# Scanning one decay product once for all blocks in a fused scan and SwiGLU kernel on one Trainium2 core

## The chip, the cores and the metric

One Trainium2 chip, one of its cores. Five engines run their own instruction streams and meet by semaphores: TensorE (PE, matmuls), VectorE (DVE), ScalarE (ACT), GpSimd (POOL) and SyncE (SP, which only issues transfers here). The metric is the device time of one launch in microseconds (us).

## What is computed

```python
# batch 4, heads H 8, seq 768, head_dim 32, d_state N 16; chunk 32
log_a = log(clip(a, 1e-6, 1));  cum = cumsum(log_a within the chunk)
M = (C_i . B_j) * exp(cum_i - cum_j) for j <= i          # in the chunk
y = M x + (C_i . state) * exp(cum_i)
state = exp(sum log_a) * state + sum_j exp(cum_end - cum_j) B_j x_j
# then, with x = y as 3072 tokens x 256 and DFF = 1536
out = (silu(x @ w_gate) * (x @ w_val)) @ w_out
```

All of it is float32. Two kinds of decay products are needed: those that multiply scores and B (called `aj` in the kernel, tile `L`) and those that multiply C (called `an`, tile `E`).

## The kernel before, in words

**Tiling.** The sequence is cut into NB = 6 blocks of P = 128 positions; a block of all four batches is T = 512 tokens. In a block the scan works on K = 2 pieces of Q = 64 positions. DFF is cut into NF = 12 units of 128. For each block PE computes, in this order of meaning: the sums for the states (`st <- xb`), the scores (`S <- Cz, bc`), the outputs of the scan (`y <- L, xb` for what lies in the piece and `y <- bc, T` for the state's part), then for each unit f the gate and the value (`gv`, two matmul groups, gate and value), and from the products the output (`po`). Blocks 4 and 5 are done together with fewer products (`px, py, pz, pr`, then `ox, oy, oz, or`), and so are the last eight units of block 3 in another form (`hx, hy, hz`).

**Weights.** They arrive as 64-bit patterns (`wNr`) that are turned into floats by a chain on two engines: `w_magnitude` (ACT, `wNw <- wNr`), `w_sign` and `w_rest` (ACT, `wNr <- wNr`; the rest partly on DVE), `w_range`, `w_shift` and `w_round` (DVE). In block 0 the units f < `WHOLE` multiply with the whole float32 weight (`gv <- xf, wNw`: two matmuls for the gate and two for the value). Every other unit uses a split into a high and a low fp32r part (`wNh`, cast on ACT, and `wNl`, a subtraction on DVE), and x split likewise (`xh`, and `hhx`, `hlx` for the low half in block 0), six matmuls each for gate and value. `gate_val` (L959) holds both ways.

**Decays.** Block 0 builds its `L` and `E` from rows that PE spreads. For blocks 1 to 5 the raw decays come in one tile `all` (`load_all`: 128 partitions, two halves `aj` and `an`, each NA x W = 3 x 65 = 195 wide), are clipped on POOL (`clip_all`), and go back to memory as `clipped` by one transfer that ACT issues (`write_all`). From there `load_aj` (two transfers a block, `L <- clipped`) and `load_an` (one, `E <- clipped`) spread them, and DVE scans them into running products: `scan_j`, four times a block, `L <- L, dj`, and `scan_n`, once a block, `E <- E, dn`, each 128 x 520. `weigh_b` multiplies B with the last decays (`xb <- xb, L`), four instructions of 128x128 a block, on POOL for block 0 and on DVE after it. `weigh_c` multiplies C (`bc <- bc, E`), `mix` the scores (`L <- S, L`), the step of the state is `T <- T, E, T` and `T <- T, E`.

**Order.** Nothing is ordered by hand. Each piece of work is added to a planner with an engine, a cost, a rank and what it needs; the planner puts it on an engine's list by its rank (a due time), and `Ordered` then fixes that list as the engine's program. All instructions are issued in that helper, L202, so every row of the trace has line 202 and is told apart by its tiles. The ranks hang on a table of numbers: `LEAD[k]` is how long before its block's units a block's scan work is due, `LATE` ties a block's loads to a weight, `AHEAD` is how early stored weights are fetched, `BEHIND` sorts the terms of the last output products, `SUM_LAG` sets the sums before them. The lines in question:

```python
add("Act", 0.45, write_all, 7.5, ["clipped"], gives="written", lag=0.6)
...
add("DVE", 1.17, do(scan_n, k), z + 6, [("an", k)], gives=("E", k), slack=1.0)
...
WHOLE = 9
```

Of the kernel before, what the change touches and what calls it, by code (L numbers as in the profile page):

```python
# [28 lines left out]
NF = DFF // P  # L29
# [14 lines left out]
class Plan:  # L44
# [26 lines left out]
    def add(self, engine, cost, run, rank, needs=(), takes=(), uses=(), gives=None, kind=None, lag=0.0, rows=1.0, slack=0.0):  # L71
        engines = [(engine, cost)] if cost is not None else engine
        self.ops.append(Op(engines, run, rank, needs, takes, uses, gives, kind, lag, rows, slack))
# [139 lines left out]
def scan_moe_kernel(ctx: ExitStack, tc, rows, decays, bc, xb, wgv, wo, cst, out):  # L213
    nc = tc.nc
    PSUM = bass.MemoryType.PSUM
    te, ve, se, ge, sp = (
        Ordered(tc, e) for e in (nc.tensor, nc.vector, nc.scalar, nc.gpsimd, nc.sync)
    )
# [18 lines left out]
    dn = const.tile([P, BATCH * K, W], F32, tag="dn", name="dn")  # L237
# [5 lines left out]
    clipped = dram.tile([2, P, NA * W], F32, name="clipped")  # L243
    bl = [dict(y={}) for _ in range(NB)]
# [50 lines left out]
        t = bl[0]["all"] = att.tile([P, 2, NA, W], F32, name="all")  # L295
        sp.dma_start(t.rearrange("p i a t -> p i (a t)"), decays.rearrange("i p c -> p i c"))

    def write_all():
        t = bl[0]["all"]
        se.dma_start(clipped.rearrange("i p c -> p i c"), t.rearrange("p i a t -> p i (a t)"))  # L300

    def load_bc(k):
        t = bl[k]["bc"] = att.tile([P, 2, BATCH, P], F32, tag="bc", name=f"bc{k}")
# [15 lines left out]
    def scan(t, d):  # L319

        ve.tensor_tensor_scan(t, t, d, 0.0, ALU.mult, ALU.add)
# [30 lines left out]
        t = bl[k]["L"][:, H * b : H * b + H]  # L352
        scan(t.rearrange("p h t -> p (h t)"), dj.rearrange("p h t -> p (h t)"))

    def scan_n(k):

        scan(bl[k]["E"].rearrange("p b q t -> p (b q t)"), dn.rearrange("p g t -> p (g t)"))


    def heads_apart(k, e):  # L360

# [6 lines left out]

    def weigh_b(k, b):

        t = bl[k]["Bj"].rearrange("p b (h n) -> p b h n", n=N)[:, b]
        L = bl[k]["L"].rearrange("p (b h) t -> p b h t", h=H)[:, b, :, Q:]
        (ve if k else ge).tensor_tensor(out=t, in0=t, in1=L.to_broadcast([P, H, N]), op=ALU.mult)

    def weigh_c(k):
        t = bl[k]["C"].rearrange("p b (q i) -> p b q i", i=Q)
# [664 lines left out]
    def do(f, *a):  # L1041
        return lambda *e: f(*a, *e)
# [6 lines left out]
    add = plan.add  # L1049

    GV, GVH, PO, ATT, FIRST, PACE0, GVP = 2.82, 2.6, 1.41, 5.0, 18.0, 3.5, 4.95
    begin, begin_sum, t = {}, {}, FIRST
# [27 lines left out]
    for n, ranks in enumerate(IDLE):  # L1080
        for i, r in enumerate(ranks):
            need = [("idle", n, i - 1)] if i else [("idle", n - 1, len(IDLE[n - 1]) - 1)] if n else []
            if n:
                need = need + [(("S", 0, BATCH - 1), ("vals", 0), ("y", 0))[n - 1]]
# [25 lines left out]

    add("SP", 0.48, load_all, 3.6, [("sent", 0)], gives="all", lag=0.6)
    add("Pool", 1.5, clip_all, 13.0, ["all", *(("bt", 0, b) for b in range(BATCH))], gives="clipped")
    add("Act", 0.45, write_all, 7.5, ["clipped"], gives="written", lag=0.6)


    for k in range(NB):
# [7 lines left out]
        def gate(key):  # L1124
            return [("asked", 1) if key in ("bc", "xb") else ("round", GATE[key])] if k == 1 else []
# [11 lines left out]
        if not k:  # L1137
            add("-", 0.0, lambda: None, -9, takes=[("x", "rows")], gives="rows", lag=0.1)
            for i in range(2):
                add("DVE", 0.2, do(clip_rows, i), -9 + i, ["rows"], gives=("clip", i))  # L1140
            for b in range(BATCH + 1):
                for i in range(2 if b < BATCH else 1):
                    t = ("spread", b, i)
                    last_one = int(i and b == BATCH - 1)
                    r = z + (3.0 if b == BATCH else 0.1 * b + i * (0.15 if b == BATCH - 1 else 0.5))
                    d = -1.09 if b == BATCH else r
                    done = ("E", 0) if b == BATCH else ("L", 0, b)
                    bank = "at" if in_at(b, i) else "mm"
                    add("PE", 0.433 if b < BATCH else 0.2, do(spread, b, i), r, [("clip", i)] + ([("S", 0, BATCH - 1)] if b == BATCH else []), takes=[(bank, t)], uses=[t, "rows"], gives=t, kind="s", slack=0.1)
                    need = [t, ("decays", 0), "dj"] + ([("scan0", b - last_one)] if i else []) + ([("M", 0, NP - 2)] if b == BATCH else [])  # L1150
                    add("DVE", 0.6, do(scan_spread, b, i), d, need, uses=[t], gives=done if i or b == BATCH else ("scan0", b))
        else:
            add("SP", 0.96, do(load_aj, k), z - 12, ["written", ("decays", k), *late, *gate("aj")], gives=("aj", k), lag={1: 5.0, 2: 11.0}.get(k, 6.0))
            plan.marked[plan.ops[-1]] = ("asked", k)
            add("SP", 0.48, do(load_an, k), z - 9, ["written", ("decays", k), *late, *gate("an")], gives=("an", k), lag=1.3)
            for b in range(BATCH):
                add("DVE", 1.14, do(scan_j, k, b), z + 0.5 + b, [("aj", k)], gives=("L", k, b), slack=2.0)
            add("DVE", 1.17, do(scan_n, k), z + 6, [("an", k)], gives=("E", k), slack=1.0)
        for b in range(BATCH):
            add(*(("DVE", 0.21) if k else ("Pool", 0.45)), do(weigh_b, k, b), z + 1.0 + b if k else -1.2, [("L", k, b), ("xb", k)], gives=("bt", k, b))  # L1160
        apart_done = [("Cz", k)]
        add([("Act", 1.25), ("DVE", 0.72)][: 1 + (k > 0)], None, do(heads_apart, k), z, [("bc", k), "cs"], takes=[("Cz", CZ)], gives=("Cz", k))
        add("DVE", 0.6 if k else 0.35, do(weigh_c, k), z + 8 if k else -1.0, [("E", k), *apart_done], gives=("ce", k))
# [3 lines left out]
        for bs in [(b,) for b in range(BATCH)] if not k else [range(BATCH)]:  # L1167
            b, more = bs[-1], bs[0]
            n = len(bs)
            stb = st[:1] if k in ST_ONE else st  # L1170
            bank = "mm" if k in ST_MM else "at"
            if k in JOINED:
                def run(k=k, bs=bs):
                    sums(k, bs)
                    scores(k, bs)
                need = [*(("bt", k, i) for i in bs), ("Cz", k)]
                add("PE", 2.04, run, z + 3, need, takes=[*((bank, i) for i in stb), *(("at", i) for i in S)], uses=[*stb, *S, CZ], gives=("S", k, BATCH - 1), kind="f", slack=SLACK)
                continue
            add("PE", 0.11 if n == 1 else 0.9, do(sums, k, bs), -1.5 if not k else z + 3, [*(("bt", k, i) for i in bs), *([("st", k, more - 1)] if more else [] if k else [("spread", BATCH - 1, 1)])], takes=[] if more else [(bank, i) for i in stb], uses=stb, gives=("st", k, b), kind="f", slack=SLACK, rows=1.0)
            add("PE", 0.214 if n == 1 else 1.25, do(scores, k, bs), z + 3.5 if k else -1.9 + 0.1 * b, ([("Cz", k), ("st", k, BATCH - 1)] if k else apart_done) + ([("S", k, more - 1)] if more else []), takes=[] if more else [("at" if k else "mm", i) for i in S], uses=[*S, CZ], gives=("S", k, b), kind="f", slack=SLACK, rows=1.0)  # L1180
        done = [("S", k, BATCH - 1)]
        add("-", 0.0, do(new_states, k), z + 2, behind("T"), takes=[("T", TT)], gives=("T", k))
# [310 lines left out]
NA = NB * K * BATCH * H // P  # L1493
IDLE = [-9.0] * 22, [-1.45] * 4, [-1.35] * 2, [1000.0] * 3
LATER = 2.4
ST_ONE, ST_MM, JOINED = (), (1, 2, 3, 4), (1, 2, 3, 4)
LEAD = {1: -26.4, 2: -36, 3: -65.3, 4: -66.7, 5: -56.2}
PAIR_LAG, MIXED, RAW = 5.0, 4, 4
MIXED_AFTER = ("y", 1)
HALVED = {3: 4}  # L1500
HALF_AT = "z"
MAKE, MAKE_STEP = 116.9, 3.3
LOOSE = {3: (3, 5, 7)}
AHEAD, URGENT = 14.6, 60


def in_raw(f):
# [2 lines left out]

OUT_MAKE, OUT_STEP = 198.7, 3.7
OUT_RAW = 1, 3, 5
BEHIND, AFTER = 0.9, 0
MORE = 3
EARLY, SUM_LAG = 7.7, 8.0
STAYS = "11", "12", "21", "22", "t1", "t2", "t4"
SPARE = ("L", 0), ("E", 0), ("bc", 0), ("xb", 0), ("Cz", 0), ("T", 0), ("T", 1), ("dj", 0), ("dn", 0), ("w", 0)
MADE = (
# [15 lines left out]
    return f >= HALVED.get(k, NF)  # L1534


WHOLE = 9
LATE = {2: NF + 2}
GATE, HASTE = dict(bc=0, aj=0, xb=0, an=1), 7
HELD = {1: ("M", 0, 0), 2: ("M", 0, 1), 3: ("M", 0, 3)}  # L1540

# [51 lines left out]
```

## Time and profile before

| | |
|---|---|
| median of 3 runs | 336.8 us (336.55 to 337.06) |
| the profiled execution | 337.27 us, of which the trace's span is 335.6 |
| PE busy | 330.7 us, 99% of the span |
| PE weight loads busy | 259.2 us, 77% |
| DVE busy | 294.8 us, 88% |
| ACT busy | 193.3 us, 58% |
| POOL busy | 4.3 us, 1% |
| granted TensorE clock | 0.998 of full |
| chain of work that ended last | PE 98%, DMA 1% |

A row of the timeline gives when an instruction started, how long it (or the xN of its kind) ran, its engine, line and operation, the tiles written and read, and in brackets the time the engine stood idle before it, with what ended that. Instructions of one engine overlap a little, so the time that one costs its engine is the distance from start to start, which is somewhat less than its duration.

### The profile page before, as it was taken

To read this page: it belongs to the slowest core of one execution; us is meant where nothing else is said; L and a number is where in the kernel's file an instruction comes from. 1 tells how busy PE (TensorE), PEld (TensorE's weight loads), DVE (VectorE), ACT (ScalarE), POOL (GpSimd) and SP (SyncE) were. 2 spreads that over 40 slices of the span, in tenths; PEclk is the share of its full clock that TensorE was granted. 3 is DMA by queue.
4 is the path that set the end of the run, shared out by engine and by line. 5 is a ranking of instruction groups with operands and counts; after the bars stand their busy time and mean duration, and the time that the engine had idled before them with its cause. 6 is when DMAs were issued, how large, how long until landed. Compare 5 with 4: busy or idle time off the path is not lost.

```text
span 335.6 us, 7902 instructions
## 1 busy us (share of the span) xinstructions
PE 330.7 (99%) x3189; PEld 259.2 (77%) x3189; DVE 294.8 (88%) x574; ACT 193.3 (58%) x360; POOL 4.3 (1%) x11
## 2 busy tenths in 40 slices
PE   8999999999999999999999999999999999999995
PEld 7544448888888888878888889988888888888784
DVE  5999999987997999887999985997578999889993
ACT  3686899276554653555455344553565556544982
POOL 1300000000000000000000000000000000000000
PEclk9999999999999999999999999999999999999999
DMA  7699749992011599277978489543036522230011
GB/s 246 185 331 343 206 127 385 289 247 64 25 33 34 163 257 368 97 278 217 274 250 305 152 279 202 188 137 118 2 125 251 190 69 69 114 125 0 1 65 63
DMA packets 21261, 57.68 MB, mean 172 GB/s; under 512 B 2280, under 2 KB 3304, under 8 KB 21224
## 3 DMA queue, kind: packets, MB, share of 16 engines
q1 hardware_dynamic: 20808, 56.94, 53.7%
q8 instruction: 25, 0.41, 0.5%
q10 hardware_dynamic: 416, 0.23, 0.2%
q14 instruction: 12, 0.10, 0.1%
HBM read 41.23 MB, written 15.93 MB: 170 GB/s over the span
## 4 chain that ended last, share of the span: by engine, by line
PE 98%; DMA 1%; ACT 0%; issue 0%; DVE 0%; ACTq 0%
PE gv L202 35%; PE po L202 20%; PE py L202 7%; PE y L202 5%; PE px L202 5%; PE oy L202 4%; PE hy L202 3%; PE pr L202 2%; PE pz L202 2%; PE ox L202 2%; PE S L202 2%; PE a L202 2%; PE hx L202 2%; PE hz L202 2%; PE st L202 1%; PE oz L202 1%
## 5 line engine op out<-in xcount | busy, mean ns | idle before, releaser
L202 ACT CAST hh<-sg 128x512 fp32r<-128x512 f32 (+1 forms) x54 | 29.2, 558 | 32.5 <-PE po L202 23.4
L202 DVE TENSOR_TENSOR hl<-sg,hh 128x512 fp32r<-128x512 f32 (+1 forms) x56 | 33.3, 607 | 7.8 <-ACT hh L202 7.5
L202 ACT ACTIVATE sg<-gv 128x512 f32<-128x512 f32 x40 | 23.8, 595 | 23.3 <-PE gv L202 19.6
L202 DVE TENSOR_TENSOR sg<-gv,sg 128x512 f32<-128x512 f32 x40 | 27.1, 678 | 2.8 <-PE gv L202 2.8
L202 DVE TENSOR_TENSOR_SCAN L<-L,dj 128x520 f32<-128x520 f32 x20 | 24.1, 1228 | 0.0
L202 DVE TENSOR_TENSOR ws<-ws 128x128 f32<-128x128 f32 (+1 forms) x60 | 19.9, 361 | 0.5 <-DMA ws<-uncut 0.4
L202 DVE TENSOR_TENSOR L<-S,L 128x512 f32<-128x512 f32 x24 | 15.7, 682 | 1.1 <-PE S L202 1.1
L202 ACT ACTIVATE sg<-px 128x512 f32<-128x512 f32 x12 | 7.2, 599 | 15.8 <-PE px L202 15.8
L202 PE MATMUL py<-xht,ws 128*128 128x512 f32 x48 | 15.3, 401 | 0.0
L202 DVE TENSOR_TENSOR hlt<-stt,hht 128x512 fp32r<-128x512 f32 x18 | 11.7, 684 | 0.9 <-ACT hht L202 0.7
L202 PEld LDWEIGHTS y<-L,xb 64*32 64x32 f32 x768 | 8.7, 105 | 4.8 <-issue 3.6
L202 ACT CAST ws<-ws 128x512 fp32r<-128x512 f32 x11 | 6.8, 622 | 8.4 <-DVE ws L202 8.2
L202 ACT ACTIVATE sg<-pz 128x512 f32<-128x512 f32 x12 | 7.2, 599 | 7.3 <-PE pz L202 7.3
L202 PE MATMUL y<-L,xb 64*32 64x64 f32 x768 | 10.9, 224 | 0.2 <-issue 0.2
L202 ACT ACTIVATE Cz<-bc,cs 128x512 f32<-128x512 f32 x12 | 8.0, 716 | 5.0 <-DMA bc<-in_bc 5.0
L202 PEld LDWEIGHTS py<-xht,ws 128*128 128x128 f32 x48 | 8.6, 188 | 2.8 <-DVE pz L202 1.2
L202 DVE TENSOR_TENSOR ps<-py,ps 128x512 f32<-128x512 f32 x12 | 8.3, 689 | 2.7 <-PE py L202 2.7
L202 ACT CAST hht<-stt 128x512 fp32r<-128x512 f32 x17 | 9.8, 622 | 0.7 <-DVE stt L202 0.6
L202 PE MATMUL py<-xlt,ws 128*128 128x512 f32 x24 | 9.4, 391 | 0.0
L202 DVE TENSOR_TENSOR pz<-py,ps 128x512 f32<-128x512 f32 x12 | 8.3, 694 | 0.7 <-PE py L202 0.4
L202 ACT COPY py<-px 128x512 f32<-128x512 f32 x12 | 6.9, 574 | 1.3
L202 PE MATMUL y<-bc,T 32*64 32x64 f32 x352 | 7.6, 223 | 0.0
(774 smaller groups left out, 979.7 us busy)
## 6 DMA issues: line engine op xcount, KB each, us to landing
ws<-keep SPq DMA_DIRECT2D x20, 512.0 KB, 4.2
keep<-ws SPq DMA_DIRECT2D x12, 512.0 KB, 5.9
L<-clipped SPq DMA_DIRECT2D x10, 520.0 KB, 10.7
xb<-in_xb SPq DMA_DIRECT2D x6, 768.0 KB, 9.4
bc<-in_bc SPq DMA_DIRECT2D x6, 512.0 KB, 10.7
ws<-uncut SPq DMA_DIRECT2D x12, 256.0 KB, 3.9
wos_k<-keep SPq DMA_DIRECT2D x6, 512.0 KB, 4.3
out<-ob SPq DMA_DIRECT2D x8, 256.0 KB, 4.7
```

Source lines behind the costliest of these rows:

```text
L202: ins = getattr(self.engine, name)(*a, **k)
```

## The change

The `an` half of `all` is scanned once, as 128 x 195, before it is written (`scan_all`, DVE), in place of a scan of each block's spread tile (`scan_n` is gone, and `load_an` now brings the finished products). `write_all` becomes two transfers, the second after that scan. `weigh_b` of blocks 1 to 5 becomes one instruction over all four batches, which needs all four scans of `L`. `WHOLE` goes from 9 to 8, so unit 8 of block 0 uses the split weights. Five settings that set ranks are new.

```diff
-    def write_all():
-        t = bl[0]["all"]
-        se.dma_start(clipped.rearrange("i p c -> p i c"), t.rearrange("p i a t -> p i (a t)"))
+    def scan_all():
+        t = bl[0]["all"][:, 1].rearrange("p a t -> p (a t)")
+        scan(t, dn[:, :NA].rearrange("p g t -> p (g t)"))
+
+    def write_all(i):
+        se.dma_start(clipped[i], bl[0]["all"][:, i].rearrange("p a t -> p (a t)"))
...
-    def scan_n(k):
-
-        scan(bl[k]["E"].rearrange("p b q t -> p (b q t)"), dn.rearrange("p g t -> p (g t)"))
...
-        t = bl[k]["Bj"].rearrange("p b (h n) -> p b h n", n=N)[:, b]
-        L = bl[k]["L"].rearrange("p (b h) t -> p b h t", h=H)[:, b, :, Q:]
-        (ve if k else ge).tensor_tensor(out=t, in0=t, in1=L.to_broadcast([P, H, N]), op=ALU.mult)
+        t = bl[k]["Bj"].rearrange("p b (h n) -> p b h n", n=N)
+        L = bl[k]["L"].rearrange("p (b h) t -> p b h t", h=H)[:, :, :, Q:]
+        if k:
+            ve.tensor_tensor(out=t, in0=t, in1=L.to_broadcast([P, BATCH, H, N]), op=ALU.mult)
+        else:
+            ge.tensor_tensor(out=t[:, b], in0=t[:, b], in1=L[:, b].to_broadcast([P, H, N]), op=ALU.mult)
...
-    add("Act", 0.45, write_all, 7.5, ["clipped"], gives="written", lag=0.6)
+    add("Act", 0.45, do(write_all, 0), 7.5, ["clipped"], gives=("written", 0), lag=0.6)
+    add("DVE", 0.47, scan_all, SCAN_ALL, ["clipped", ("xf", 2 * K - 1)], gives="scanned")
+    add("Act", 0.45, do(write_all, 1), 7.6, ["scanned"], gives=("written", 1), lag=0.6)
...
-            add("SP", 0.48, do(load_an, k), z - 9, ["written", ("decays", k), *late, *gate("an")], gives=("an", k), lag=1.3)
+            add("SP", 0.48, do(load_an, k), z - 9, [("written", 1), ("decays", k), *late, *gate("an")], gives=("E", k), lag=1.3)
...
-            add("DVE", 1.17, do(scan_n, k), z + 6, [("an", k)], gives=("E", k), slack=1.0)
...
+            add("DVE", 0.6, do(weigh_b, k, 0), z + 4.0, [*(("L", k, b) for b in range(BATCH)), ("xb", k)], gives=("bt", k, BATCH - 1))
...
+SCAN_ALL = 1.0
-LEAD = {1: -26.4, 2: -36, 3: -65.3, 4: -66.7, 5: -56.2}
+LEAD = {1: -27.1, 2: -40.4, 3: -64.2, 4: -67.5, 5: -56.2}
-AHEAD, URGENT = 14.6, 60
+AHEAD, URGENT = 13.1, 60
-BEHIND, AFTER = 0.9, 0
+BEHIND, AFTER = 0.6, 0
-EARLY, SUM_LAG = 7.7, 8.0
+EARLY, SUM_LAG = 7.7, 4.1
-WHOLE = 9
-LATE = {2: NF + 2}
+WHOLE = 8
+LATE = {2: NF + 1}
```

The first place is on DVE, ahead of the first units of block 0. `L202 ISA` is `w_round`, which unit 1's matmuls wait for. Before:

```order
L202 COPY xf<-y_1_263 128x4x64
L202 COPY xf<-y_1_306 128x4x64
L202 CAST xh_377<-xf 128x512 x2
L202 TENSOR_SCALAR wg1w<-wg1w 128x512
L202 TENSOR_TENSOR hhx<-xf,xh_377 128x512
L202 SCALAR_TENSOR_TENSOR wg1w<-wg1w,wg1r 128x512
L202 TENSOR_TENSOR hlx<-xf,xh_377 128x512
L202 ISA wg1w<-wg1r,wg1w 128x1024
```

And of the change:

```order
L202 COPY xf<-y_1_263 128x4x64
L202 COPY xf<-y_1_306 128x4x64
L202 SCALAR_TENSOR_TENSOR all<-all,dn 128x195
L202 CAST xh_383<-xf 128x512
L202 TENSOR_SCALAR wg1w<-wg1w 128x512
L202 CAST xh_383<-xf 128x512
L202 TENSOR_TENSOR hhx<-xf,xh_383 128x512
L202 SCALAR_TENSOR_TENSOR wg1w<-wg1w,wg1r 128x512
L202 TENSOR_TENSOR hlx<-xf,xh_383 128x512
```

The scan of `all` stands ahead of everything that unit 1's weight still needs from DVE; otherwise one cast of `xh` and the range have changed places.

The second place is on DVE later in block 0, where block 1's scores are mixed; the four `L<-S` rows are `mix`. Before:

```order
L202 SCALAR_TENSOR_TENSOR E_370<-E_370,dn 128x520
L202 TENSOR_TENSOR sg_6_530<-gv_6_1_527,sg_6_530 128x512
L202 ISA wg8w<-wg8r,wg8w 128x1024
L202 TENSOR_SCALAR wg9w<-wg9w 128x512
L202 TENSOR_TENSOR bc_391<-bc_391,E_370 128x512
L202 SCALAR_TENSOR_TENSOR wg9w<-wg9w,wg9r 128x512
L202 TENSOR_TENSOR L_369<-S_0_572,L_369 128x4x2x64
L202 SCALAR_TENSOR_TENSOR T_108<-T_107,E_370,T_108 128x64 x4
L202 TENSOR_TENSOR L_369<-S_1_573,L_369 128x4x2x64
L202 ISA wg9w<-wg9r,wg9w 128x1024
L202 TENSOR_TENSOR L_369<-S_2_574,L_369 128x4x2x64
L202 TENSOR_TENSOR sg_7_636<-gv_7_1_633,sg_7_636 128x512
```

And of the change:

```order
L202 ISA wg8w<-wg8r,wg8w 128x1024
L202 ISA wg9w<-wg9r,wg9w 128x1024
L202 TENSOR_TENSOR bc_392<-bc_392,E_370 128x512
L202 TENSOR_TENSOR L_369<-S_0_563,L_369 128x4x2x64
L202 SCALAR_TENSOR_TENSOR T_108<-T_107,E_370,T_108 128x64 x4
L202 TENSOR_TENSOR sg_6_600<-gv_6_1_609,sg_6_600 128x512
L202 TENSOR_TENSOR wg8l<-wg8w,wg8h 128x512
L202 TENSOR_TENSOR L_369<-S_1_564,L_369 128x4x2x64
L202 TENSOR_TENSOR L_369<-S_2_565,L_369 128x4x2x64
L202 SCALAR_TENSOR_TENSOR T_108<-T_108,E_370 128x64 x4
L202 TENSOR_TENSOR L_369<-S_3_566,L_369 128x4x2x64
L202 TENSOR_TENSOR sg_7_646<-gv_7_1_641,sg_7_646 128x512
```

The scan of `E` is gone, `wg8l` stands ahead of the second mix, and unit 7's product stands behind the last mix rather than ahead of it.

The third place is SP's list of transfers in the same stretch (the row with + is new there, the one with - was there before):

```order
 L202 DMA wg7r<-in_wgv 128x1024
 L202 DMA wg8r<-in_wgv 128x1024
-L202 DMA E_370<-clipped 128x1x520
 L202 DMA wg9r<-in_wgv 128x1024
 L202 DMA wg10r<-in_wgv 128x1024
 L202 DMA wg11r<-in_wgv 128x1024
+L202 DMA E_370<-clipped 128x1x520
 L202 DMA wo0r<-in_wo 128x1024
```

The spread of block 1's `E` is asked for behind three weights that it stood ahead of. On PE, the sums and scores of block 1 move from between units 6 and 7 to between unit 6's gate and value.

## Rows read from the trace of the kernel before

**Rows 1.** The page: busy time, share of the span and instructions by engine.

```profile
PE 330.7 (99%) x3189; PEld 259.2 (77%) x3189; DVE 294.8 (88%) x574; ACT 193.3 (58%) x360; POOL 4.3 (1%) x11
```

**Rows 2.** Windows: busy time by engine, clock, DMA share, GB/s.

```profile
15.00:25.00 10.00, 9.93 (x44) 4.30 (x37) 9.87 (x24) 8.99 (x17) 0.00 (x0) 1.00 0.96 313
35.00:60.00 25.00, 25.00 (x381) 15.35 (x380) 24.95 (x53) 22.35 (x45) 0.00 (x0) 1.00 0.73 242
60.00:300.00 240.00, 240.00 (x2287) 198.75 (x2287) 210.81 (x418) 126.43 (x235) 0.00 (x0) 1.00 0.55 171
```

**Rows 3.** Waits of PE: total, times, longest, in us.

```profile
PE oy L202 <- ACT oby L202: 0.5, 1, 0.5
```

**Rows 4.** Timeline of PE, units of block 0 and the first of block 1.

```profile
15.91 3.67 PE L202 MATMUL gv<-xf,wg0w 128*128 128x512 f32 x8
19.65 3.67 PE L202 MATMUL gv<-xf,wg1w 128*128 128x512 f32 x8
...
36.90 3.60 PE L202 MATMUL gv<-xf,wg6w 128*128 128x512 f32 x8
...
45.88 3.60 PE L202 MATMUL gv<-xf,wg8w 128*128 128x512 f32 x8
49.41 1.05 PE L202 MATMUL y<-L,xb 64*32 64x64 f32 x64
50.39 0.69 PE L202 MATMUL y<-bc,T 32*64 32x64 f32 x32
...
55.33 0.86 PE L202 MATMUL y<-L,xb 64*32 64x64 f32 x64
56.11 0.69 PE L202 MATMUL y<-bc,T 32*64 32x64 f32 x32
...
60.95 0.61 PE L202 MATMUL gv<-xh,wg0h 128*128 128x512 f32 x2
...
63.67 0.61 PE L202 MATMUL gv<-xh,wg1h 128*128 128x512 f32 x2
```

**Rows 5.** Timeline of DVE, ahead of unit 1 and at block 1's first scan.

```profile
15.34 0.76 DVE L202 COPY xf<-y 128x256 f32<-128x256 f32 x2
...
18.82 0.69 DVE L202 CUSTOM_DVE_ANT_0 wg1w<-wg1r,wg1w 128x1024 uint16<-128x1024 uint16 x1
...
29.70 1.23 DVE L202 TENSOR_TENSOR_SCAN L<-L,dj 128x520 f32<-128x520 f32 x1
30.85 0.67 DVE L202 TENSOR_TENSOR sg<-gv,sg 128x512 f32<-128x512 f32 x1
```

**Rows 6.** Tile E and tile xb: duration ns min/median/max, first and last start.

```profile
L202 DVE TENSOR_TENSOR_SCAN E<-E,dn x5: 1216/1229/1234, 40.4 to 218.2; 128x520 f32<-128x520 f32 x5
L202 DVE TENSOR_TENSOR_SCAN E<-a,dn x1: 689/689/689, 12.4 to 12.4; 128x260 f32<-128x260 f32 x1
...
L202 DVE TENSOR_TENSOR xb<-xb,L x20: 260/282/293, 32.4 to 218.0; 128x128 f32<-128x128 f32 x20
```

**Rows 7.** Timeline of ACT, from unit 1's weight to the first silu.

```profile
15.66 1.27 ACT L202 ACTIVATE wg1r<-wg1r 128x512 int32<-128x512 int32 x2
17.90 0.60 ACT L202 ACTIVATE sg<-gv 128x512 f32<-128x512 f32 x1 [0.97 <-PE gv L202]
```

**Rows 8.** Timeline of DVE, block 1's scores.

```profile
43.02 0.68 DVE L202 TENSOR_TENSOR bc<-bc,E 128x512 f32<-128x512 f32 x1
...
44.97 0.87 DVE L202 SCALAR_TENSOR_TENSOR T<-T,E,T 128x64 f32<-128x64 f32 x4
...
48.94 0.68 DVE L202 TENSOR_TENSOR L<-S,L 128x512 f32<-128x512 f32 x1
```

**Rows 9.** Transfers, 12 to 48 us: KB each, median us from issue to landing; SP timeline.

```profile
wg11r<-in_wgv SPq DMA_DIRECT2D x1, 512.0 KB, 11.9
wo0r<-in_wo SPq DMA_DIRECT2D x1, 512.0 KB, 3.3
...
29.49 0.33 SPq L202 DMA_DIRECT2D wg11r<-in_wgv  x1
```

More of the change, by code (lines that the diff above doesn't have):

```diff
@@ L1152, in scan_moe_kernel @@
         else:
-            add("SP", 0.96, do(load_aj, k), z - 12, ["written", ("decays", k), *late, *gate("aj")], gives=("aj", k), lag={1: 5.0, 2: 11.0}.get(k, 6.0))
+            add("SP", 0.96, do(load_aj, k), z - 12, [("written", 0), ("decays", k), *late, *gate("aj")], gives=("aj", k), lag={1: 5.0, 2: 11.0}.get(k, 6.0))
             plan.marked[plan.ops[-1]] = ("asked", k)
-            add("SP", 0.48, do(load_an, k), z - 9, ["written", ("decays", k), *late, *gate("an")], gives=("an", k), lag=1.3)
+            add("SP", 0.48, do(load_an, k), z - 9, [("written", 1), ("decays", k), *late, *gate("an")], gives=("E", k), lag=1.3)
             for b in range(BATCH):
                 add("DVE", 1.14, do(scan_j, k, b), z + 0.5 + b, [("aj", k)], gives=("L", k, b), slack=2.0)
-            add("DVE", 1.17, do(scan_n, k), z + 6, [("an", k)], gives=("E", k), slack=1.0)
-        for b in range(BATCH):
-            add(*(("DVE", 0.21) if k else ("Pool", 0.45)), do(weigh_b, k, b), z + 1.0 + b if k else -1.2, [("L", k, b), ("xb", k)], gives=("bt", k, b))
+        if k:
+            add("DVE", 0.6, do(weigh_b, k, 0), z + 4.0, [*(("L", k, b) for b in range(BATCH)), ("xb", k)], gives=("bt", k, BATCH - 1))
+        for b in range(0 if k else BATCH):
+            add("Pool", 0.45, do(weigh_b, k, b), -1.2, [("L", k, b), ("xb", k)], gives=("bt", k, b))
         apart_done = [("Cz", k)]
@@ L1175, in run @@
                     scores(k, bs)
-                need = [*(("bt", k, i) for i in bs), ("Cz", k)]
+                need = [("bt", k, BATCH - 1), ("Cz", k)]
                 add("PE", 2.04, run, z + 3, need, takes=[*((bank, i) for i in stb), *(("at", i) for i in S)], uses=[*stb, *S, CZ], gives=("S", k, BATCH - 1), kind="f", slack=SLACK)
                 continue
-            add("PE", 0.11 if n == 1 else 0.9, do(sums, k, bs), -1.5 if not k else z + 3, [*(("bt", k, i) for i in bs), *([("st", k, more - 1)] if more else [] if k else [("spread", BATCH - 1, 1)])], takes=[] if more else [(bank, i) for i in stb], uses=stb, gives=("st", k, b), kind="f", slack=SLACK, rows=1.0)
+            add("PE", 0.11 if n == 1 else 0.9, do(sums, k, bs), -1.5 if not k else z + 3, [("bt", k, b), *([("st", k, more - 1)] if more else [] if k else [("spread", BATCH - 1, 1)])], takes=[] if more else [(bank, i) for i in stb], uses=stb, gives=("st", k, b), kind="f", slack=SLACK, rows=1.0)
             add("PE", 0.214 if n == 1 else 1.25, do(scores, k, bs), z + 3.5 if k else -1.9 + 0.1 * b, ([("Cz", k), ("st", k, BATCH - 1)] if k else apart_done) + ([("S", k, more - 1)] if more else []), takes=[] if more else [("at" if k else "mm", i) for i in S], uses=[*S, CZ], gives=("S", k, b), kind="f", slack=SLACK, rows=1.0)
```

## The prediction

> **What bounds the kernel.** I read four views, in this order. The page comes first: PE is busy for 330.7 of 335.6 us, DVE for 294.8 [rows 1]. Then the windows, to see whether that is an average over stages: from 60 to 300 us PE is busy for 240.00 of 240.00 us, at a granted clock of 1.00, while DVE has 29 us to spare in them [rows 2]. Between 35 and 60 us DVE is full too, 24.95 of 25.00, and from 15 to 25 us it is at 9.87 of 10.00 [rows 2]: there the two run neck and neck, and DVE can decide. Third, the waits: the one worth a name behind 60 us is 0.5 us before the last output products, on an ACT copy [rows 3]. Last, the timeline of PE, because a matmul's busy time is modelled and its start isn't. The whole units 1 to 5 start 17.25 / 5 = 3.45 us apart, while each shows 3.60 to 3.67 us of busy time [rows 4]. Unit 1 is the exception: it starts 3.74 behind unit 0, so PE already stands some 0.29 us there. Unit 1's round on DVE starts at 18.82 and takes 0.69, to 19.51, and the matmuls start at 19.65 [rows 4, 5]: 0.14 behind it, so DVE sets that start. So PE is the path from 16 us to the end; a change counts where it alters PE's own work, and where DVE is late for it before 60 us.
>
> **What the change does, part by part.**
>
> *Unit 8 by split weights* is the one change of PE's work. A whole unit takes 3.45 from start to start; a split unit 63.67 - 60.95 = 2.72, though it has 12 matmuls for 8 [rows 4]. That is **-0.73 us**, on the path. Block 0's split units have the low half of x in two pieces of one matmul each, as units 9 to 11 have already. Moved sums, scores and y's are the same matmuls elsewhere; they cost PE nothing unless they come before their inputs.
>
> *The scan of all.* No row shows a scan 195 wide, so I go by its neighbours: 520 wide takes 1229 ns, 260 wide 689 [rows 6], so (1229 - 689) / 260 = 2.08 ns an element, and 195 wide takes 689 - 65 x 2.08 = 554 ns. From start to start a scan takes 0.08 less than its duration (29.70 to 30.85 is 1.15, for 1.23) [rows 5], which leaves 0.47. It stands right behind the copies into `xf` (15.34) and ahead of everything that unit 1's weight needs on DVE, where DVE has 0.13 us of idle time in 10 [rows 2, 5]. So unit 1's round ends at 19.51 + 0.47 = 19.98 and its matmuls start at 20.12: **+0.47**. The bounds are 0 (a gap on DVE that I don't see takes it up) and 0.61 (a scan that is not cheaper than one 260 wide: 0.689 less the 0.08). I take the value between, which is nearest to the slope of the two rows. A gain has no place here.
>
> *The second write* waits on ACT for this scan, and unit 1's sign and rest are queued behind it. They start at 15.66 now [rows 7]. The scan ends near 16.6 and an issue takes 0.33 [rows 9], so they start near 17.0; the two take 1.27 and end near 18.3, the sign some 0.6 before, ahead of the round at 19.3 and of DVE's shift, which stands two instructions of 0.6 before it. Unit 0's silu behind them has 0.97 us of idle time before it [rows 7], so it slips by some 0.4 us. I put it at nothing; without that cover it would cost what ACT is late, up to 1.3 (17.0 less 15.66).
>
> *The five scans of E go, and the twenty weighings become five.* The scans were 5 x 1.15 = 5.8 us of DVE [rows 6]. Twenty weighings of 0.28 become five 512 wide, which I put at 0.68 each from C's weighing of the same width (43.02) [rows 6, 8]: 5.6 less 3.4, and with 0.08 of overlap for each instruction 1.0 rather than 2.2. With the new scan, DVE loses 5.8 + 1.0 - 0.47 = 6.3 of 294.8 us. Behind 60 us that is worth nothing, since PE has no gap to close there [rows 2]. The bound that costs: a weighing that now needs all four scans of L comes late for sums that have moved ahead. In block 1 the sums would start at 36.90 + 1.72 + 0.47 = 39.09 (half a unit into unit 6) [rows 4], and by DVE's new order the weighing ends near 38.2, so 0.9 us remain. In blocks 2 and 4, where the sums come one and two pairs of products earlier, I find some 2 us. Zero, then.
>
> *Block 1's y.* One place before 60 us does gain. The first part of y takes 50.39 - 49.41 = 0.98 from its start to the next, at 55.33 the same 64 matmuls take 0.78 [rows 4], because the last mix starts at 48.94 and ends at 49.62 [rows 8], inside it: **-0.20**. Ahead of that mix DVE loses the scan of E (1.15), 0.2 of weighing and unit 7's product (0.6, now behind it), and gains 0.47 of the new scan and 0.6 of `wg8l`: 0.9 earlier, while y itself starts 0.73 - 0.47 = 0.26 earlier. So the wait goes. What is late next there is `wg8l`: unit 8 starts at 45.88 + 0.47 = 46.35 and wants it two matmuls later, near 46.8. Its chain is the weighing of C, a mix, the state's step, unit 6's product and `wg8l`: four of 0.68 and one of 0.87, less 0.08 each, are 3.2 [rows 8]. C's weighing is at 43.02 now; with the scan of E and the rest gone from ahead of it I put it near 42.4, so `wg8l` ends near 45.6 to 45.8, 1 us ahead.
>
> *Block 1's E* moves behind three weights in SP's queue. Its bytes still come from the same sum of bytes, so what stands last lands when wg11r does now, at 29.49 + 11.9 = 41.4 [rows 9]; the weighing of C needs it near 42.4, and PE notices from about 43.05. Covered by 1.6 us, with the least certainty of all the covers.
>
> *The settings* move fetches and sums behind 60 us; the last stages keep the order they have, with the 0.5 us wait [rows 3]. Nothing.
>
> The **sum** is -0.73 + 0.47 - 0.20 = -0.46 us. The profiled execution took 337.27, so it would take 336.81; the median of the runs shown, 336.8, lies 0.47 below that execution, so **336.3 us**. A measurement of this kernel can tell about 0.2% (0.67 us) from no change, so this is within it.
>
> **The rivals.**
>
> *The new scan is hidden.* If DVE catches up before unit 1's round, the 0.47 goes and 336.3 - 0.47 = 335.9 comes out, faster by 0.27%. For it: 0.13 us of idle time in this window, and two rows that have changed places. Against it: those 0.13 don't hold 0.47. Chance 0.26.
>
> *Unit 8's low part comes late.* Then the split unit gains nothing, 336.3 + 0.73 = 337.1, no change that can be told. For it: DVE is full from 35 to 60 [rows 2]; against it, the 1 us above. Chance 0.09.
>
> *E of block 1 comes late*, the one that ends on the other side. DVE's list is in order, so a late E holds the weighing of C and behind it the first mix, unit 6's product and `wg8l`; unit 8 and then y wait. If its bytes don't move until wg11r has landed at 41.4, and take what wo0r took on an empty queue (3.3) [rows 9], E is there at 44.7, 1.65 behind the 43.05 from which it decides: 336.3 + 1.65 = 338.0. It is slower by over 0.2% from a landing near 44.2. For it: a DMA share of 0.96 up to 25 us and 11.9 us for a weight. Against it: no row says that transfers wait for one another in full, and 1.6 us of cover. Chance 0.12. [...]
>
> *DVE is the bound where PE looks full.* Busy PE could hide starts that wait for DVE, in the two stretches where DVE is saturated; each would give back the 1.35 us that a block's scan and weighing take off DVE: 336.3 - 2 x 1.35 = 333.6. Against it: whole units at even distances with 3.60 us shown busy in 3.45 [rows 4]. Chance 0.03. [...]
>
> **How the numbers follow.** The forecast has 0.50; its own range is 336.0 to 336.9 (the bounds of the new scan, y's 0.20, and 0.25 us by which medians of such runs differ), of which 0.07 lies below 336.8 - 0.67 = 336.1 and 0.43 within. Faster: 0.07 + 0.26 + 0.03 = 0.36. Within 0.2%: 0.43 + 0.09 = 0.52. Slower: 0.12. The range goes from 335.7, under the hidden scan, to 337.4, over the late low part with its 0.25; it leaves out the late E and the DVE bound, 0.15 together, and little else.
>
> **What would show it.** In the new profile: a scan 128x195 of about 0.55 us on DVE near 16 us; unit 1's matmuls starting near 20.1 and 0.14 behind their round; unit 8 as twelve matmuls over 2.7 us; y's first part 0.78 long; PE at 240.00 from 60 to 300; DVE near 288.5 us in all. The hidden scan shows as unit 1 at 19.65. A wait of PE on `wg8l`, or of DVE on E, ahead of unit 8 makes it wrong upwards; starts of PE that draw together behind 60 us, or a wait of over half a us anywhere in the pair of blocks, would make my reading of PE's rows wrong.

## The result and the profile after

The changed kernel takes 340.78 us in the median of 22 runs (336.61 to 344.71), the kernel before 337.06 (336.19 to 338.97). The ratios here and below leave out as slow a kernel's runs that are over 1.5% above its fastest (here five, 341.73 and more). This one is 1.0077, 95% interval 1.0054 to 1.0101: slower by 0.8%, or by 1.1% by the two medians, where 336.3 us was forecast. The single runs fall into groups: three lie at 336.6 to 336.9, four at 338.15 to 338.88, and fifteen at 340.35 or more. The execution that was profiled first is one of the three (336.61 us), so its page shows the change at its best, and the loss isn't in it.

The page's busy times and the waits of PE in that execution:

```profile
PE 328.7 (98%) x3190; PEld 259.4 (77%) x3193; DVE 288.8 (86%) x555; ACT 193.4 (58%) x360; POOL 4.2 (1%) x11
```

```profile
...
PE gv L202 <- DVE wg1w L202: 0.5, 1, 0.5
...
PE oy L202 <- ACT oby L202: 0.5, 1, 0.5
PE gv L202 <- DVE sg L202: 0.4, 1, 0.4
```

DVE lost 6.0 us of work (294.8 to 288.8), PE's time hardly changed, and PE now names a wait for unit 1's weight. The timeline of PE in the same execution, the rows that answer to [rows 4]:

```profile
15.22 3.67 PE L202 MATMUL gv<-xf,wg0w 128*128 128x512 f32 x8
19.42 3.67 PE L202 MATMUL gv<-xf,wg1w 128*128 128x512 f32 x8 [0.53 <-DVE wg1w L202]
...
36.66 1.88 PE L202 MATMUL gv<-xf,wg6w 128*128 128x512 f32 x4
38.47 0.86 PE L202 MATMUL st<-xb 64*32 64x64 f32 x64
39.26 1.21 PE L202 MATMUL S<-Cz,bc 32*64 32x128 f32 x64
40.39 1.98 PE L202 MATMUL gv<-xf,wg6w 128*128 128x512 f32 x4
42.21 3.60 PE L202 MATMUL gv<-xf,wg7w 128*128 128x512 f32 x8
45.24 1.03 PE L202 MATMUL gv<-xh,wg8h 128*128 128x512 f32 x2
...
48.48 0.95 PE L202 MATMUL y<-L,xb 64*32 64x64 f32 x64
49.37 0.69 PE L202 MATMUL y<-bc,T 32*64 32x64 f32 x32
```

And DVE ahead of unit 1, answering to [rows 5]:

```profile
15.32 0.55 DVE L202 TENSOR_TENSOR_SCAN all<-all,dn 128x195 f32<-128x195 f32 x1
15.79 0.40 DVE L202 CAST xh<-xf 128x512 fp32r<-128x512 f32 x1
...
18.59 0.68 DVE L202 CUSTOM_DVE_ANT_0 wg1w<-wg1r,wg1w 128x1024 uint16<-128x1024 uint16 x1
```

The scan takes 0.55 and 0.47 from its start to the next, as worked out. In distances, which leave out that unit 0 starts at 15.2 to 15.9 in different executions:

| from start to start | before | after | change | forecast |
|---|---|---|---|---|
| unit 0 to unit 1 | 3.74 | 4.20 | +0.46 | +0.47 |
| unit 1 to block 1's y | 29.76 | 29.06 | -0.70 | -0.73 |
| y's first part | 0.98 | 0.89 | -0.09 | -0.20 |
| unit 0 to block 1's first unit | 45.04 | 44.72 | -0.32 | -0.46 |

Unit 7 stands here in the kernel before:

```profile
42.35 3.70 PE L202 MATMUL gv<-xf,wg7w 128*128 128x512 f32 x8
```

From unit 7's start to y, units 7 and 8 take 7.06 us before and 6.27 after, 0.79 less; unit 6 with the sums and scores takes 5.45 and 5.55, 0.10 more.

Up to 60 us, then, the change does about what was forecast of it. The rest of the kernel decides.

### The profile page after: what moved, and what is told of

It reads as the page before. It is cut to its first block, busy times and chain, and to the rows that moved or that the text cites. A ratio compares the mean times of both kernels' runs of the same rounds, so it can differ in the third digit from the quotient of the medians.

```text
span 334.9 us, 7895 instructions
## 1 busy us (share of the span) xinstructions
PE 328.7 (98%) x3190; PEld 259.4 (77%) x3193; DVE 288.8 (86%) x555; ACT 193.4 (58%) x360; POOL 4.2 (1%) x11
## 4 chain that ended last, share of the span: by engine, by line
PE 91%; DVE 3%; DMA 3%; ACT 1%; issue 1%; SPq 0%; DVEq 0%; ACTq 0%
PE gv L202 31%; PE po L202 20%; PE py L202 7%; PE px L202 5%; PE y L202 4%; PE oy L202 4%; PE hy L202 3%; PE pz L202 2%; PE pr L202 2%; PE ox L202 2%; DMA ws<-uncut 2%; PE hx L202 2%; PE hz L202 2%; PE S L202 2%; DVE L L202 2%; PE oz L202 1%
## 5 line engine op out<-in xcount | busy, mean ns | idle before, releaser
L202 ACT CAST hh<-sg 128x512 fp32r<-128x512 f32 (+1 forms) x54 | 29.2, 557 | 29.9 <-PE po L202 23.1
L202 DVE TENSOR_TENSOR hl<-sg,hh 128x512 fp32r<-128x512 f32 (+1 forms) x56 | 33.3, 615 | 8.4 <-ACT hh L202 8.4
L202 ACT ACTIVATE sg<-gv 128x512 f32<-128x512 f32 x40 | 23.9, 598 | 26.2 <-PE gv L202 26.0
L202 DVE TENSOR_TENSOR sg<-gv,sg 128x512 f32<-128x512 f32 x40 | 27.6, 690 | 5.0 <-PE gv L202 5.0
L202 DVE TENSOR_TENSOR_SCAN L<-L,dj 128x520 f32<-128x520 f32 x20 | 24.3, 1232 | 0.0
L202 DVE TENSOR_TENSOR ws<-ws 128x128 f32<-128x128 f32 (+1 forms) x60 | 20.1, 370 | 0.7 <-DMA ws<-uncut 0.6
L202 DVE TENSOR_TENSOR L<-S,L 128x512 f32<-128x512 f32 x24 | 15.8, 689 | 3.0 <-PE S L202 3.0
L202 ACT ACTIVATE sg<-px 128x512 f32<-128x512 f32 x12 | 7.2, 599 | 15.9 <-PE px L202 15.9
L202 PE MATMUL py<-xht,ws 128*128 128x512 f32 x48 | 15.3, 400 | 0.0
L202 DVE TENSOR_TENSOR hlt<-stt,hht 128x512 fp32r<-128x512 f32 x18 | 11.7, 689 | 0.9 <-ACT hht L202 0.7
L202 PEld LDWEIGHTS y<-L,xb 64*32 64x32 f32 x768 | 8.6, 105 | 4.3 <-issue 3.5
L202 DVE TENSOR_TENSOR ps<-py,ps 128x512 f32<-128x512 f32 x12 | 8.3, 690 | 3.7 <-PE py L202 3.7
L202 ACT CAST ws<-ws 128x512 fp32r<-128x512 f32 x10 | 6.2, 622 | 8.9 <-DVE ws L202 8.8
L202 ACT ACTIVATE sg<-pz 128x512 f32<-128x512 f32 x12 | 7.2, 599 | 7.0 <-PE pz L202 7.0
L202 PE MATMUL y<-L,xb 64*32 64x64 f32 x768 | 10.7, 224 | 0.2 <-issue 0.2
L202 PEld LDWEIGHTS py<-xht,ws 128*128 128x128 f32 x48 | 8.6, 188 | 2.7 <-DVE pz L202 1.2
L202 ACT ACTIVATE Cz<-bc,cs 128x512 f32<-128x512 f32 x12 | 8.0, 716 | 4.7 <-DMA bc<-in_bc 4.7
L202 ACT CAST hht<-stt 128x512 fp32r<-128x512 f32 x17 | 9.7, 619 | 0.7 <-DVE stt L202 0.6
L202 PE MATMUL py<-xlt,ws 128*128 128x512 f32 x24 | 9.4, 390 | 0.0
L202 DVE TENSOR_TENSOR pz<-py,ps 128x512 f32<-128x512 f32 x12 | 8.4, 696 | 0.7 <-PE py L202 0.3
L202 ACT COPY py<-px 128x512 f32<-128x512 f32 x12 | 6.9, 572 | 2.0 <-PE px L202 0.7
L202 ACT COPY ob<-po 128x512 f32<-128x512 f32 x8 | 4.7, 587 | 5.7 <-PE po L202 5.3
```

Of the source, the lines that this page charges most:

```text
L202: ins = getattr(self.engine, name)(*a, **k)
```

## The experiments

Every time is a median of its runs unless it says a single run. Runs that were made together share a chip and the runs of the kernel before.

**The changed kernel again, two single runs, and two partial undoings.** The first repeat:

> The changed kernel once more, to catch an execution near its median (340.8 us) in a profile; the one profiled so far took 336.61. Theory 1 (a transfer that lands late): one wait of PE of 2 to 5 us stands in the trace behind a DMA, either block 1's E ahead of unit 8 (40 to 47 us) or a stored weight coming back for block 3 (150 to 160 us), and the rest of PE's starts keep their distances. Theory 2 (the clock falls without a wait): no wait over 0.6 us, but stretches with a granted clock under 0.95. Theory 3 (PE's work is longer in many places): waits of DVE products on PE spread over all stages, none over 0.6 us.

The second repeat:

> The same kernel a second time. If theory 1 holds, the late place is the same one as in the other look wherever the time is over 338 us, and the length of the wait follows the time: the time less 336.6 within 0.5 us.

The first took 337.14 us without a new wait. The second took 340.95 and holds the loss. PE's waits there:

```profile
PE S L202 <- issue: 2.4, 1, 2.4
```

and its timeline at block 4's sums and scores:

```profile
176.32 0.86 PE L202 MATMUL st<-xb 64*32 64x64 f32 x64
177.11 1.19 PE L202 MATMUL S<-Cz,bc 32*64 32x128 f32 x63
180.66 0.32 PE L202 MATMUL S<-Cz,bc 32*64 32x128 f32 x1 [2.36 <-issue]
180.91 0.79 PE L202 MATMUL po<-hh,wo2h 128*128 128x512 f32 x1
181.50 0.63 PE L202 MATMUL po<-hl,wo2h 128*128 128x512 f32 x1
```

63 of 64 scores run, the last one waits 2.36 us, and the profile names nothing that it waits for ("issue" is time in which an engine waits for nothing that the profile shows). The output products behind it start some 0.43 us apart rather than 0.23. From block 4's first score to the last instruction the second repeat takes 162.13 us, the first 157.88: 4.25 lost, 2.36 by the wait and the rest behind it. Theory 1 has the size of the wait right, but neither of its two places is hit, and no transfer of data is named.

What PE lacks can be read from the transfers. A queue of instructions, q8, moves 25 packets over the whole span, on the changed kernel's page:

```profile
q8 instruction: 25, 0.41, 0.5%
```

0.41 MB in 25 packets is 16 KB each, and PE's 6383 rows (matmuls and weight loads) over 25 are 255 instructions to a packet. The page doesn't name q8's engine; that it is PE's is inferred, here and below, from how its packets go with PE's count and PE's waits. During output products PE uses two of them in 0.227 us, a packet in 29 us. The sums and scores of a block are 128 matmuls and 128 weight loads in 1.92 us: a whole packet. In the first profiled execution, from 172 to 178 us:

```profile
q8 instruction: 1, 0.02, 1.0%
```

In the second repeat there is none from 150 to 178 us, and one from 178 to 180 us:

```profile
q8 instruction: 1, 0.02, 2.9%
```

Counted in the records, the packet starts at 178.36 there, when PE has issued 3996 matmuls and weight loads and stands; PE goes on 2.30 us after that start. In the two executions without the wait (336.61 and 337.14 us) it starts at 173.04 and 173.53, when PE has issued 3714 and 3717. So in this execution PE seems to run out of instructions at block 4's last score. That became theory F, against a rival D, that the score waits for data or a bank that the trace doesn't name.

The undoings, both on the changed kernel:

```diff
-LEAD = {1: -27.1, 2: -40.4, 3: -64.2, 4: -67.5, 5: -56.2}
-LATE = {2: NF + 1}
+LEAD = {1: -26.4, 2: -36, 3: -65.3, 4: -66.7, 5: -56.2}
+LATE = {2: NF + 2}
```

> The change with the old leads of the blocks' scan work and the old tie of block 2's loads, so that loads, sums and scores stand about where they stood before; whole units still 8, one scan of C's products. If the new leads bring the late transfer: 336.3 to 337.0 median, each run within 1 us. If the structure does it (the products scanned once, two writes, E spread later, weighing in one go): 340 to 341 as the changed kernel.

```diff
-WHOLE = 8
+WHOLE = 9
```

> The change with nine whole units again. If unit 8's split form with its late low part brings the lost time: 337.0 (336.3 plus 0.7) and little spread. If leads or structure do: 340 to 342, spread as in the changed kernel.

Old leads: 336.65 us (12 runs, 336.18 to 339.84), ratio to the kernel before 0.999 (0.9968 to 1.0013). Nine whole units: 337.17 (11 runs, 336.76 to 338.18), 0.9994 (0.9982 to 1.0005). Both lose the group at 340, but for one run of the old leads at 339.84, so neither the structure alone nor unit 8 alone makes it. But both lists are planned anew by such an edit: in both, the three stored weights that SP asks for together at 170.4 us in the change are not asked for there any more (SP's rows have such transfers between 157 and 165 us), and with the old leads the scores stand elsewhere. They say that order matters, not which order. (Of the settings, `AHEAD`, `BEHIND`, `SUM_LAG` and `LATE` move no instruction on any engine when they are set back; the leads and `WHOLE` do.)

**Three ways to pull theory F and rival D apart, and the scan moved.** The first plans the three transfers behind block 4's scores; PE's, DVE's and ACT's lists stay as they are:

```diff
+            if k in HALVED and f - HALVED[k] >= HOLD_FROM:
+                need.append(("S", PAIR, BATCH - 1))
...
+HOLD_FROM = 3
```

> The changed kernel with three transfers moved: the three stored weights that SP asks for together at 170.4 us now wait for block 4's scores. PE's program is the same instruction for instruction. Theory F (PE runs out of instructions, because the 16 KB packet with its next ones lies behind those transfers): the packet starts near 173.5 in every run, no wait in the scores, median 336.6 to 337.2 and no run over 339. Rival D (the last score waits for data or a bank that the trace doesn't name): nothing that the score reads or writes has moved, so 340 to 341 with waits of 2 to 3 us at the same instruction.

The second puts more instructions at PE's start, so that the borders between packets fall elsewhere:

```diff
+        if not n and i == len(IDLE[0]) - 1:
+            for j in range(PAD):
+                q, p = 0, j % NP
+                te.matmul(rest[0][pair(p), Q * q : Q * q + Q], one[piece(q), pair(p)], one[piece(q), :Q], start=True, stop=True)
...
+PAD = 72
-IDLE = [-9.0] * 22, [-1.45] * 4, [-1.35] * 2, [1000.0] * 3
+IDLE = [-9.0] * 14, [-1.45] * 4, [-1.35] * 2, [1000.0] * 3
```

> The changed kernel with 128 more instructions at PE's start (72 tiny matmuls and their weight loads in place of 8 of the 22 warm-up ones; no transfer and nothing else moves). Theory F: the border between two packets moves from the last score of block 4 to about the first one, and the packet behind it is asked for 128 instructions, some 14 us, earlier, before the three transfers: no wait there, median 336.6 to 337.4 (unless another burst meets a border now, which would show as a wait of the same kind elsewhere). Rival D: 340 to 341, the wait at the last score as before.

The third sets block 4's lead alone back, `4: -67.5` to `4: -66.7`. Up to block 4's scores every engine's list is that of the change; there, half a pair of output products comes ahead of the sums:

> The changed kernel with block 4's old lead alone: its sums and scores come half a pair of products (six matmuls, 1.36 us) later, the transfers ahead of them stay. Theory F: a packet that is 5 us late now finds PE 1.4 us less far, so the wait shrinks from 2.4 to about 1.0 us, median 337.5 to 339.5. If the lead of block 4 has no part in it: 340 to 341. Theory of a lead that starts it all: 336.6.

The fourth, with the old leads, gives `scan_all` one more need, `("round", 1)`:

> The old leads, and the scan of C's products behind unit 1's round rather than ahead of it. This measures the term that was forecast at +0.47: unit 1 starts 3.74 us behind unit 0 as in the kernel before, not 4.20, and the median is 0.4 to 0.5 below that of the old leads alone (336.65), near 336.2. Rival: the scan only moves the same 0.47 to unit 2, whose weight is next in DVE's list; then unit 2 starts 3.9 behind unit 1 and the median stays at 336.6.

*Transfers held:* 336.57 us (12 runs, 336.06 to 338.13), ratio 0.9972 (0.9949 to 0.9995), no run at 340. SP asks for the three 0.4 us before the first score, where it was 6.7 us. Nothing that the score reads or writes was moved; rival D falls.

One part of F's forecast missed: the packet doesn't start near 173.5. It starts at 177.15, when PE is at 3741, and in the later run of the same kernel at 176.12, again at 3741. That is only just early enough. In both, PE takes up the last score 2.30 and 2.27 us after the packet's start, behind a gap of 0.2 us that the two good executions of the change don't have. The scores are stretched by it; here, and in the first repeat of the change:

```profile
178.31 1.46 PE L202 MATMUL S<-Cz,bc 32*64 32x128 f32 x64
```

```profile
177.55 1.21 PE L202 MATMUL S<-Cz,bc 32*64 32x128 f32 x64
```

So the same score follows the packet by the same 2.3 us whether it waits 2.36 us or 0.2, which is what F says; D has no reason for it. In both profiles the packet starts within 5 ns of the end of the last data packet under way. While it runs, no data move (busy time by engine, granted clock, DMA share, GB/s):

```profile
177.20:178.00 0.80, 0.80 (x50) 0.48 (x52) 0.80 (x3) 0.37 (x1) 0.00 (x0) 1.00 0.00 0
```

That speaks for a packet that waits behind data, here behind transfers other than the three.

*More instructions:* 341.14 us (6 runs, 340.31 to 343.43). Block 4's scores run without a wait, as F has it, but every run is over 340, since the exception that the expectation allowed for came true: another burst meets a border. PE's timeline, at block 0's y:

```profile
13.72 0.71 PE L202 MATMUL y<-L,xb 64*32 64x64 f32 x47
17.60 0.53 PE L202 MATMUL y<-L,xb 64*32 64x64 f32 x17 [3.17 <-issue]
```

and PE's instruction queue from 15 to 16.2 us:

```profile
q8 instruction: 1, 0.02, 4.8%
```

Nothing but PE's instruction count was changed, and the nameless wait went from 178 us to 14 us, with its packet beside it (it starts at 15.10, 2.50 us before PE goes on). D has no way to do that. My median for this run was wrong.

*Block 4's old lead:* 336.70 us (12 runs, 335.75 to 337.13), ratio 0.9965 (0.9945 to 0.9985). The wait didn't shrink to 1.0, it is gone. The slack of 1.4 us isn't what the traces show at work: the packet starts at 172.02, when PE is at 3715, before the lists part (near 176.4), and at 172.68 in the later run of the same kernel. Both are executions in which it came early, and why none of the runs meets a late one stays open.

*The later scan:* unit 1 starts 3.74 us behind unit 0 again and unit 2 another 3.54 behind it (3.51 in the change), so the 0.47 is the scan's and is not handed on. The median, 337.16 (336.18 to 340.74), shows no gain, since two of twelve runs took 340.7. The profiled one of those has another cause, which the timeline of DVE shows:

```profile
31.98 1.24 DVE L202 TENSOR_TENSOR_SCAN L<-L,dj 128x520 f32<-128x520 f32 x1 [1.82 <-DMA L<-clipped]
...
36.91 0.43 DVE L202 TENSOR_SCALAR wg7w<-wg7w 128x512 f32<-128x512 f32 x1 [1.36 <-ACT wg7w L202]
```

Block 1's decays and then a weight land late, DVE's list stands behind them, and PE waits 2.6 us ahead of block 1's sums, which start at 42.70, right behind the weighing of B (41.91, 0.68 long).

**A third repeat, and both repairs.**

> The changed kernel a third time. Theory F (PE runs out of instructions in block 4's scores): if the time is over 339, the wait stands at the same score, the 63rd or 64th, with nothing named behind it, and the packet with PE's next instructions starts near 178 us; if it is under 337.5, the packet starts near 173 and there is no wait.

It took 338.34 us, between the two cases, and has a wait of neither kind. PE waits 1.4 us for a product, because DVE stands ahead of it for a weight that is fetched back, 1.69 us here; in the kernel before, the same wait took 0.4 us and PE didn't notice:

```profile
157.84 0.29 DVE L202 TENSOR_TENSOR ws<-ws 128x128 f32<-128x128 f32 x1 [1.69 <-DMA ws<-uncut]
158.05 0.68 DVE L202 TENSOR_TENSOR sg<-gv,sg 128x512 f32<-128x512 f32 x1
```

The profile with the held transfers has it as well (1.86 us of DVE, 1.6 of PE). Block 4's old lead with the later scan:

> The change with block 4's old lead and with the scan of C's products behind unit 1's round: the two repairs together. If the 0.46 us that unit 1 loses stays gained: near 336.2 (336.7 less 0.46), unit 1 starting 3.74 us behind unit 0, no packet late at block 4. If block 1's burst, which moves half a unit later and closer to the border that the late scan with the old leads met in two of twelve runs, is hit: single runs near 340 and a median that says nothing.

336.45 in the profiled run, with unit 1 at 3.74, but 338.14 in the median of 12 runs from 335.92 to 340.58, ratio 1.0028 (0.9999 to 1.0057). The unfavourable branch came true. The profiled run shows how near block 4's border still is: the packet starts at 176.71 there, and PE stands ahead of the 60th score, which follows 2.3 us after:

```profile
179.01 0.44 PE L202 MATMUL S<-Cz,bc 32*64 32x128 f32 x5 [0.23 <-issue]
```

So block 4's old lead doesn't by itself bring the packet early. None of its runs over 337 us is in a profile, so which transfer or packet is late in them stays open.

**The change and both repairs on one chip.** The runs so far were made on several chips; these were made together on one, to take away the doubt that the chips differ.

> The changed kernel, timed beside both repairs on one chip. Theory F: most runs at 340 to 342 (the missing packet, 2.4 us, and a slower clock behind it), the rest between 336.5 and 339 (no wait, or the late weight alone). If the session made the difference: 336.5 to 337.5 here.

> Block 4's old lead alone, again. Theory F: no run in the 340 to 342 group; median 336.5 to 337.2, 3.5 to 4 us below the changed kernel. If the session made the difference: the same times as the changed kernel, group for group.

> Three transfers held, PE's program that of the change, again. Theory F: no run in the 340 to 342 group; single runs at 337.5 to 338.5 where the returning weight is late (1.6 us in the profile of its first session), median 336.5 to 337.2. If the session made the difference: the same times as the changed kernel.

| one chip, 12 runs each | median | lowest to highest | ratio to before |
|---|---|---|---|
| the change | 339.19 | 336.54 to 341.99 | 1.0038 (1.0008 to 1.0068); 1.006 by the medians |
| block 4's old lead | 336.45 | 336.06 to 337.54 | 0.998 (0.9964 to 0.9996) |
| three transfers held | 336.85 | 336.06 to 337.37 | 0.9983 (0.9964 to 1.0001) |

Nine of twelve runs of the change are at 338.49 or more, none of the 24 with a repair is. The group at 340 is smaller than expected (four runs), and there are five at 338.49 to 339.57.

The mean granted clock of every run tells the two apart. It is 0.990 to 0.993 in the four, and 0.998 or more in the other eight. Of the 22 runs at the start, thirteen of the fifteen at 340 have 0.988 to 0.995, the other two (340.35 and 340.38 us) 0.999. No run of the change under 340, and none of the 48 with one of these two repairs, is under 0.997. A low mean goes with a long pause of PE, not with this one alone: the two profiles with 2.36 us have 0.993, that of the later scan, with its other wait of 2.6 us, has 0.995. So the five at 338.49 to 339.57, like the two at 340.35 and 340.38, don't show the mark of the pause, and no profile of them was taken. Block 4's old lead has none like them, though its lists part from the change's only at block 4's scores; that most of the five lose their time there or later is inferred, not shown, and the third repeat (338.34 us) lost its time before. The profiled run of the change, at 340.93 us, has the same wait at the same score:

```profile
177.18 1.19 PE L202 MATMUL S<-Cz,bc 32*64 32x128 f32 x63
180.74 0.32 PE L202 MATMUL S<-Cz,bc 32*64 32x128 f32 x1 [2.36 <-issue]
```

Its windows (busy time by engine, granted clock, DMA share, GB/s):

```profile
172.00:178.00 6.00, 6.00 (x140) 4.89 (x145) 6.00 (x12) 3.52 (x7) 0.00 (x0) 1.00 0.96 287
178.00:182.00 4.00, 1.64 (x31) 1.08 (x18) 2.97 (x8) 0.89 (x4) 0.00 (x0) 0.90 0.97 372
182.00:186.00 4.00, 4.00 (x14) 3.19 (x13) 1.50 (x4) 0.94 (x2) 0.00 (x0) 0.68 0.02 8
```

The first profiled execution of the change, at 336.61 us:

```profile
172.00:178.00 6.00, 6.00 (x146) 4.89 (x146) 6.00 (x12) 3.53 (x8) 0.00 (x0) 1.00 0.98 301
```

Block 4's old lead, and then the held transfers:

```profile
172.00:178.00 6.00, 6.00 (x87) 4.79 (x87) 6.00 (x12) 3.59 (x6) 0.00 (x0) 1.00 0.98 318
...
182.00:186.00 4.00, 4.00 (x20) 3.30 (x19) 4.00 (x13) 0.62 (x1) 0.00 (x0) 1.00 0.02 6
```

```profile
172.00:178.00 6.00, 6.00 (x135) 4.85 (x138) 6.00 (x12) 3.53 (x7) 0.00 (x0) 1.00 0.50 191
```

In the change the transfers are at 0.96 of their time in the six microseconds in which PE's next packet is needed; held, at 0.50. With the old lead they are as full (0.98), and in the good execution of the change too (0.98); yet the packet starts at 172.68 and 173.04 in these. So full queues alone don't make it late. Behind the wait the granted clock is 0.68 over 4 us, and in the second repeat it stands at 0.50 for most of that:

```profile
181.00:184.30 3.30, 3.30 (x8) 2.62 (x9) 0.00 (x0) 0.37 (x1) 0.00 (x0) 0.50 0.21 78
```

The products start 0.43 us apart up to 184.4, nearly twice their 0.227, after 2.36 us in which PE did nothing. The wait is 2.36 and what follows costs nearly as much again.

## Why the prediction was wrong

*The views and the bound.* Right: PE is the path, and DVE decides up to 60 us. Behind block 1's first unit, what DVE lost (6.3 us from 60 to 300 us, 210.81 to 204.51) brings nothing: 274.60 us to the end before, 274.77 in the first repeat of the change, which has no large wait. Ahead of it, the rival that DVE is the bound wanted 2.7 us and 0.32 came, so it is out.

*Unit 8, the scan of all, the second write, y.* Right in sign and nearly in size: +0.46 for +0.47. From unit 1 to y the change gains 0.70 for 0.73: 0.79 on units 7 and 8, less 0.10 on unit 6, which is now cut in two by the sums and scores. y's wait shrank by 0.09, not 0.20. ACT's write stood from 15.91 to 16.24; the sign behind it started at 16.28, 1.06 behind unit 0 (1.1 forecast), and DVE's row shows no wait for it.

*E of block 1.* Covered, as said: DVE stands ahead of block 1's weighing of C, which reads E, in no profile. In the first one it starts at 41.22, 26.0 us behind unit 0, for 26.5 forecast. The 43.05 from which a late E was to cost PE isn't worked out from any row. The rival on the other side had a late transfer in mind and the wrong one; where E lands no run here shows.

*The moved sums.* This step failed: "In blocks 2 and 4, where the sums come one and two pairs of products earlier, I find some 2 us. Zero, then." The 2 us were counted against what the sums read. What they also need is themselves: 256 instructions, and where PE stood for a packet it went on only 2.27 to 2.50 us after the packet's start. With a lead larger by 0.8 us they come half a pair of products earlier, and in two profiled executions at 341 us PE waits 2.36 us at the last score for the packet with its next instructions, and loses 1.9 more behind the wait. 17 of the 19 runs at 340 or more (15 of 22 and 4 of 12) have the low clock that goes with such a pause. Set back alone, that one number takes the change from 339.19 to 336.45 on one chip; I put it, with all the settings, at nothing.

*The sum.* -0.46 against the kernel before, on a base of three runs (336.8) that twenty-two put at 337.06. With that number set back it is 336.45 to 337.2, -0.75, within the forecast's own reach. The range (335.7 to 337.4) holds the medians of both repairs and misses the change as it is: no rival said that PE could run out of instructions, and "a wait of over half a us anywhere in the pair of blocks" was named as what would make the reading wrong, though not this wait. Nor did I ask how a kernel whose runs spread over 3 us answers to a list that is tighter: a forecast from one execution can't show a loss that some executions have and others don't.

That PE waits for this packet is shown; why the packet is late is shown in part. With the transfers held it starts at 176.12 and 177.15, just as the last data packet ends, and in the executions at 341 us amid transfers that fill the queues: both fit a packet that lies behind data. But the queues are as full in good executions, and it starts at 173.04 there. The records give its start and not when it is asked for, so what decides between the two, and why block 4's old lead has it early in both its profiles, stays open.

## What to carry to other kernels

Where an engine runs many small instructions in a burst, count them against its instruction packets: here a block's sums and scores used up a whole packet, 256 instructions, in 1.92 us, and where PE stood it went on 2.3 to 2.5 us after the start of the next. Ask too what large transfers are planned ahead of the burst: on one chip the change took 339.19 us, and 336.85 with three transfers held back. A wait that the profile can't name ("issue"), in the middle of equal instructions (2.36 us at the last of 64 scores), together with a late packet on the engine's instruction queue (starting at 178.36 in place of 173.04 us), was the sign of it. And when the runs of a kernel fall into groups, take a profile of each group before you explain a median.

## What the hardware showed that was not expected

PE's instructions come in packets of 16 KB, 255 to a packet (0.41 MB and 6383 rows over 25 packets, on the changed kernel's page). In a good execution of the change (the first repeat) the packet starts when PE is at 3717, and PE needs it at 3996, 279 later, about one packet ahead: 5.0 us here. In six profiles PE stands for a packet, for 0.2 to 3.2 us, and goes on 2.27 to 2.50 us after the packet's start. While the packet runs in the two executions at 341 us, the data packets under way fall from 16.3 to 15.4 in the mean. At the border between two packets PE stood 2.36 us there, and 3.17 with more instructions ahead. A pause of PE of 2.36 us was followed by 4 us at a granted clock of 0.68; in the second repeat pause and low clock cost 4.25 us together.
